# Reordering the first two halves of a fused attention and feed-forward kernel: copies ahead of norms, more banks, selects for the global rows, loads and fills in another order

## The chip, the cores and the metric

The kernel runs on one core of one Trainium2 chip. The metric is device time in microseconds (us) of one execution, lower is better. Within one round of measurements the executions of the kernel before lie within 1.5 to 1.7% of one another. A few executions were of a slower state: one of the kernel before in four of the five rounds of experiments (265.98 to 266.10 us) and one of m9 (269.40 us). Ratios and intervals use the fast ones alone, medians are over all. The rounds ran on different chips; where medians of two rounds are subtracted below, the kernel before moved by under 1 us between them (263.76 to 264.59). Engines are named as in the profile: PE is TensorE, DVE is VectorE, ACT is ScalarE, POOL is GpSimd, SP is SyncE, and SPq or ACTq is the part of an engine that issues DMAs.

## The reference

Windowed attention with a few global keys and a distance bias, followed by a gated feed-forward layer. Cut to what matters:

```python
# q, k, v: (4 batches, 8 heads, 768 positions, 64); n_global = 8; n_local = 96
scores = q @ k.T / sqrt(64)
is_global = key_pos < 8
is_local = (rel >= 0) & (rel < 96)                 # rel = query_pos - key_pos
dist = where(is_global & ~is_local, 96, abs(rel))
scores += -slope[head] * dist                      # slope = 2 ** -(head + 1)
a = softmax(where(is_global | is_local, scores, -1e9))
x = (a @ v) as (3072 tokens, 512)
out = (maximum(x @ w_gate, 0) * (x @ w_val)) @ w_out     # 512 -> 1536 -> 512
```

## The kernel before

A sequence of 768 queries is worked in two halves of 384, so there are eight "halves", numbered here from the first to the eighth (in the code from 0 to 7). Attention of a half goes by four pairs of heads. A helper `weave` lays feed-forward products of one half between attention pieces of a later one. The program is scheduled by hand: the order of these Python calls is the order of each engine's instructions. Some words used below: a *cast* turns float32 into bf16; a *norm* is the last step of a head pair's attention, the product with the inverse of the sum of the exps; a *product* is one tile of a feed-forward layer's first stage, four matmuls; *banks* are the tiles that matmuls write into; *fills* are memsets.

The third half belongs to the second batch, which has value and key buffers of its own (`vbuf[1]`, `kT[1]`). Each value tile starts with the eight global rows. They are loaded once, into tile 0, and then spread to the other tiles by DMAs inside the chip's memory:

```python
def spread_v_globals(b, j0=1, j1=NT):
    for j in range(j0, j1):
        nc.sync.dma_start(out=v_dst(b, 0, NG, j), in_=v_dst(b, 0, NG, 0))

def load_v_half(s):
    b, half = divmod(s, 2)
    if half == 0:
        load_v_globals(b)
        spread_v_globals(b)                 # issued by SP
    for j in range(4) if half == 0 else range(4, NT):
        load_v(b, j)                        # issued by POOL

def load_qk_after(s, by_pairs=False):       # loads that a small DVE memset holds back
    ...
        nc.vector.memset(t[0:1, 0:H:step, 0:1], 0.0)
    ...
```

From the third half on, keys and queries are not transposed by PE but by DMA. POOL casts them, SP issues the transposes, and POOL lays the keys in place:

```python
def early_pieces(s):
    out = [(0.0, lambda p=p: piece_cast_k(s, p)) for p in range(HP)]    # POOL: kc <- ks
    out += [(0.0, lambda n=n: piece_xk(s, n)) for n in range(NN)]       # SP: kN <- kc transposed
    out += [(0.0, lambda p=p: piece_cast_q(s, p)) for p in range(HP)]   # POOL: qz <- qs
    out += [(0.0, lambda n=n: piece_xq(s, n)) for n in range(NN)]       # SP: qT <- qz transposed
    out += [(0.0, lambda p=p: piece_order(s, p)) for p in range(HP)]    # POOL: kT <- kN
    return out
```

The end of the program's setup:

```python
weave(f1_0[G[0]] + f1_0[G[1]], spread(att1, 0.05, 0.95), ...)   # second half's attention
for p in range(HP):
    nc.gpsimd.memset(kT[1][p][...], 0)                          # two of them
nc.gpsimd.memset(vbuf[1][:, NT - 1, :]..., 0)                   # last value tile of batch 1
for j in range(NT):
    fill_ones(nc.gpsimd, 1, j)                                  # ones beside the values
for i in range(2):
    nc.gpsimd.memset(qz[i]..., 0)
load_qk_after(2)
load_w(wo_sb, moe_w_out, 0, DM)
load_v_half(2)                                                  # behind the fills
weave(f1_1[G[0]] + f1_1[G[1]], ...)
weave(f1_0[G[2]] + f1_1[G[2]], spread(early_pieces(2), 0.0, 1.0))
load_qk(3, 0, H)
load_v_half(3)                                                  # behind the transposes
weave(f2_0 + f2_1, spread(attention_pieces(2), 0.0, 0.85), spread(early_pieces(3), 0.2, 0.8))
```

The softmax here doesn't subtract the row's maximum and nothing guards it: scores larger than these inputs give would overflow.

## Time and profile before

| | before |
|---|---|
| time, median of 4 runs beside the changed kernel | 264.59 us (262.21 to 266.27) |
| span of the profiled run, mean granted PE clock | 261.9 us, 0.98 |
| first half's last norm, second half's last norm | 26.22 us, 47.01 us |
| third half: POOL's casts of keys, PE reaches its attention | 56.62 us, 69.59 us |
| gap at 90 us | 2.1 us idle, then 3.2 us at half clock |

Timeline columns: start, duration, engine, line, operation, output<-input, count, and in brackets the idle time ahead and what ended it.

### The profile page before, as it was taken

What the parts mean: (1) busy time and instruction counts of PE and PEld (TensorE: products, weight loads), DVE (VectorE), ACT (ScalarE), POOL (GpSimd) and SP (SyncE); (2) the same over time, 40 slices, a digit from 0 to 9 for tenths busy, and PEclk for the clock granted to TensorE, in tenths of its full rate; (3) what the DMA queues carried; (4) which work ended last, traced back from release to release, by engine and by line L of the source; (5) the groups of instructions that cost most, each with busy time, mean ns of one, the idle gap of its engine ahead of it and who ended that gap; (6) DMA issues with size and microseconds to landing.
All of it is one profiled execution on the core that took longest, in us unless ns stands there. A gap on an engine that the chain in (4) does not pass through costs nothing.

```text
span 261.9 us, 4707 instructions
## 1 busy us (share of the span) xinstructions
PE 240.1 (92%) x1637; PEld 141.6 (54%) x1646; DVE 137.2 (52%) x351; ACT 155.5 (59%) x321; POOL 94.8 (36%) x230
## 2 busy tenths in 40 slices
PE   5664997999998789999999999999999999999994
PEld 2453654566554346655665566655665566556641
DVE  7623796664353337752767167635674366714410
ACT  4165589433477538755776477756875677653321
POOL 8970895026664607710344515800640000000000
PEclk9898899999999979999999999999999999999999
DMA  6999689975994993673753994945681200021012
GB/s 180 183 186 254 148 147 156 185 227 116 245 209 116 189 294 91 138 52 117 240 108 76 125 290 95 144 62 179 183 127 55 80 3 1 3 80 40 0 43 80
DMA packets 82695, 34.36 MB, mean 131 GB/s; under 512 B 58608, under 2 KB 79600, under 8 KB 82672
## 3 DMA queue, kind: packets, MB, share of 16 engines
q1 hardware_dynamic: 50816, 26.16, 37.2%
q0 software_dynamic: 31856, 7.91, 31.1%
q8 instruction: 13, 0.21, 0.3%
q14 instruction: 10, 0.08, 0.1%
HBM read 28.38 MB, written 6.29 MB: 132 GB/s over the span
## 4 chain that ended last, share of the span: by engine, by line
PE 77%; ACT 7%; DVE 7%; DMA 4%; issue 1%; POOL 1%; SPq 1%; POOLq 0%; ACTq 0%
PE ff_ps L472 22%; PE ff_ps L462 21%; PE ff_ps L481 21%; PE qk_ps L366 5%; PE av_ps L394 4%; DMA qT<-qz 2%; DVE xT L411 2%; PE av_ps L425 1%; ACT grelu L465 1%; ACT es L319 1%; DVE ht L474 1%; DMA qs<-in_q_dram 1%; ACT es L369 1%; ACT lnd L435 1%; DMA kN<-kc 1%
## 5 line engine op out<-in xcount | busy, mean ns | idle before, releaser
L472 PE MATMUL ff_ps<-xT,wv 128*128 128x384 bf16 x384 | 78.9, 328 | 0.6 <-DVE ht L474 0.3
L462 PE MATMUL ff_ps<-xT,wg 128*128 128x384 bf16 x384 | 79.3, 330 | 0.0
L465 ACT ACTIVATE grelu<-ff_ps 128x384 bf16<-128x384 f32 x96 | 47.1, 490 | 39.8 <-DVE ht L474 21.0
L474 DVE TENSOR_TENSOR ht<-ff_ps,grelu 128x384 bf16<-128x384 f32 x96 | 53.3, 555 | 27.1 <-PE ff_ps L472 22.6
L481 PE MATMUL ff_ps<-wo_sb,ht 128*128 128x512 bf16 x279 | 66.6, 379 | 0.5
L378 DVE TENSOR_TENSOR es<-es,m_all 128x432 bf16<-128x432 bf16 (+6 forms) x128 | 39.1, 338 | 28.7 <-ACT es L369 28.0
L369 ACT ACTIVATE es<-qk_ps 128x432 bf16<-128x432 f32 (+2 forms) x84 | 43.6, 532 | 12.9 <-PE qk_ps L366 11.5
L472 PEld LDWEIGHTS <-wv 128*128 128x128 bf16 x384 | 36.5, 99 | 23.8 <-issue 2.8
L462 PEld LDWEIGHTS <-wg 128*128 128x128 bf16 x384 | 36.6, 98 | 23.4 <-issue 1.2
L411 DVE TENSOR_TENSOR xT<-av_ps,rcp 64x384 bf16<-64x384 f32 x48 | 26.7, 555 | 43.0 <-ACT rcp L408 38.0
L481 PEld LDWEIGHTS <-ht 128*128 128x128 bf16 x288 | 26.9, 97 | 27.9
L322 POOL CAST kc<-ks 128x384 bf16<-128x384 f32 x24 | 12.3, 555 | 64.5 <-DMA ks<-in_k_dram 64.5
L366 PE MATMUL qk_ps<-qT,kT 128*128 128x432 bf16 (+6 forms) x128 | 28.6, 289 | 2.9 <-DMA qT<-qz 2.1
L403 ACT ACTIVATE lnd<-av_ps 64x384 f32<-64x384 f32 x48 | 23.3, 485 | 10.6 <-PE av_ps L394 10.0
L486 ACT COPY osb<-ff_ps 128x512 f32<-128x512 f32 x24 | 14.1, 586 | 25.3 <-PE ff_ps L481 24.5
L130 POOL DMA_DIRECT2D vbuf<-in_v_dram x28 | 24.3, 876 | 0.8 <-issue 0.7
L394 PEld LDWEIGHTS <-vbuf 128*128 128x128 bf16 x216 | 18.0, 98 | 8.8 <-issue 1.5
L394 PE MATMUL av_ps<-es,vbuf 128*128 128x216 bf16 (+4 forms) x216 | 21.1, 226 | 1.1 <-DVE xT L411 0.8
L366 PEld LDWEIGHTS <-kT 128*128 128x128 bf16 x128 | 12.5, 99 | 12.9 <-issue 2.8
L330 POOL CAST qz<-qs 128x192 bf16<-128x192 f32 x48 | 14.5, 353 | 4.6 <-DMA qs<-in_q_dram 4.4
L408 ACT ACTIVATE rcp<-lnd 128x384 f32<-128x384 f32 x24 | 12.5, 523 | 0.8
L319 ACT ACTIVATE es<-qk_ps 128x432 bf16<-128x432 f32 (+1 forms) x12 | 5.2, 504 | 12.4 <-PE qk_ps L314 12.4
(74 smaller groups left out, 128.5 us busy)
## 6 DMA issues: line engine op xcount, KB each, us to landing
out_dram<-osb SPq DMA_DIRECT2D x24, 256.0 KB
ks<-in_k_dram SPq DMA_DIRECT2D x6, 768.0 KB
qs<-in_q_dram SPq DMA_DIRECT2D x6, 768.0 KB
vbuf<-in_v_dram POOLq DMA_DIRECT2D x24, 120.0 KB, 6.8
ks<-in_k_dram SPq DMA_DIRECT2D x8, 192.0 KB
qs<-in_q_dram SPq DMA_DIRECT2D x8, 192.0 KB
wg<-in_moe_w_gate_dram POOLq DMA_DIRECT2D x3, 512.0 KB, 7.1
wv<-in_moe_w_val_dram POOLq DMA_DIRECT2D x3, 512.0 KB, 9.0
```

What stands on the lines that cost most here:

```text
L130: nc.gpsimd.dma_start(out=v_dst(b, NG + r0, NG + r0 + n, j), in_=v[b, :, KT * j + r0 : KT * j + r0 + n, :].rearrange("h p d -> p h d"))
L366: nc.tensor.matmul(ps[:, c : c + n_], lhsT=kt[:, j, :], rhs=qd[:, :, :, a : a + w], start=True, stop=True)
L369: nc.scalar.activation(es[:, 0:cols], ps[:, 0:cols], AF.Exp, bias=0.0, scale=scale)
L378: nc.vector.tensor_mul(e4, e4, mk)
L394: nc.tensor.matmul(av3[:, :, a : a + w], lhsT=vb[:, j, z0 : z0 + 128], rhs=es[:, c : c + NN * w].rearrange("k (n p) -> k n p", n=NN), star ...
L403: nc.scalar.activation(ln[o0 : o0 + 64], av[d0 : d0 + 64, 0:QH], AF.Ln, bias=0.0, scale=1.0)
L411: nc.vector.tensor_tensor(xT_of[s][r, p, :], av_of[s, p, e_][r, 0:QH], rc[r], op=ALU.mult)
L462: nc.tensor.matmul(psg[:, 0:QH], lhsT=w_of(wg, dc, fc), rhs=xT[:, dc, :], start=(dc == 0), stop=(dc == N_DC - 1))
L465: nc.scalar.activation(gr, psg[:, 0:QH], AF.Relu, bias=0.0, scale=1.0)
L472: nc.tensor.matmul(psv[:, 0:QH], lhsT=w_of(wv, dc, fc), rhs=xT[:, dc, :], start=(dc == 0), stop=(dc == N_DC - 1))
L474: nc.vector.tensor_tensor(ht[:, fc, :], psv[:, 0:QH], st["gr"], op=ALU.mult)
L481: nc.tensor.matmul(ps2, lhsT=ht[:, fc, n * 128 : (n + 1) * 128], rhs=wo_sb[:, fc, :], start=(fc == 0), stop=(fc == N_FC - 1))
```

## The change

Its intent: shorten the chain at the start (masks of the global rows without DVE, casts and copies ahead of the norms, six banks for scores), start feed-forward products before the first half's last norm, and get every load out earlier. The diff, cut to its core:

```diff
-    def setup_global_rows():            # 7 DVE instructions on 8x216, 2 iotas
+    nc.gpsimd.affine_select(...)        # 4 selects write dd[0:NG]
+    def copy_v_globals(eng, b, j0, j1): # first batch: value rows by DVE, no DMA
...
-        banks = [qk_psum.tile(...) for _ in range(3)]
+        pool, name = (ff_psum, "ff_ps") if s == 0 and p % 2 else (qk_psum, "qk_ps")
+        banks = [pool.tile([128, 512], FP32, name=name) for _ in range(3)]
...
-    weave(f1_0[G[0]] + f1_0[G[1]], spread(att1, 0.05, 0.95), [(0.5, lambda: load_w_group(2))])
+    for f in F0[0:3]: f(0, LAST)        # three products all but their last matmul
+    piece_av_wide(0, 3); piece_norm_wide(0, 3)
+    load_w_group(1)
+    for p in range(HP): cast(1, p, P, P)
+    ...                                 # second half's pieces and 9 products by hand
+    load_qk_after(2)
+    for h in (0, 1, 6, 7): setup_mask(h)
+    load_w(wo_sb, moe_w_out, 0, DM)
+    load_v_half(2)                      # now ahead of the fills
     for p in range(HP):
         nc.gpsimd.memset(kT[1][p]..., 0)
     nc.gpsimd.memset(vbuf[1][:, NT - 1, :]..., 0)
+    for i in range(2): nc.gpsimd.memset(qz[i]..., 0)
     for j in range(NT): fill_ones(nc.gpsimd, 1, j)
-    load_qk_after(2)
-    load_w(wo_sb, moe_w_out, 0, DM)
-    load_v_half(2)
-    weave(f1_1[G[0]] + f1_1[G[1]], ...)
-    weave(f1_0[G[2]] + f1_1[G[2]], spread(early_pieces(2), 0.0, 1.0))
     load_qk(3, 0, H)
     load_v_half(3)                      # now ahead of early_pieces(2)
-    weave(f2_0 + f2_1, spread(attention_pieces(2), 0.0, 0.85), spread(early_pieces(3), 0.2, 0.8))
+    weave(f1_1[G[0]] + f1_0[G[1]][4:] + f1_1[G[1]], ..., spread(early_pieces(2), 0.5, 1.0))
+    weave(f1_0[G[2]] + f1_1[G[2]] + f2_0 + f2_1,
+          spread(attention_pieces(2), 0.2, 0.92), spread(early_pieces(3), 0.1, 0.6))
```

## The prediction

> **What bounds the kernel now.** I read the page's slices first, then a table of windows, then the list of waits for the tensor engine (PE), then the timeline around its two worst gaps. The slices are 6.5 us each:
>
> ```profile
> PE   5664997999998789999999999999999999999994
> PEclk9898899999999979999999999999999999999999
> DMA  6999689975994993673753994945681200021012
> ```
>
> From the sixteenth slice on PE is busy 90% or more and its clock is full: the steady state, one half-sequence every 28 us or so, is PE bound, and the change leaves that loop alone. What can be won lies before 96 us: the first four slices (5, 6, 6, 4 tenths), the dip in slices 13 to 15, and the slices with a reduced clock (8 tenths in the second, fourth and fifth, 7 in the fifteenth). The windows (columns: PE, weight load, DVE, ACT, POOL busy us with counts, then clock, DMA share, GB/s) measure it:
>
> ```profile
> 15.00:20.00 5.00, 2.62 (x39) 2.00 (x36) 1.82 (x6) 2.65 (x6) 2.69 (x4) 1.00 1.68 180
> 20.00:25.00 5.00, 2.03 (x28) 1.65 (x29) 2.19 (x9) 2.42 (x7) 0.00 (x0) 0.92 1.21 232
> 26.00:46.90 20.90, 18.41 (x189) 11.42 (x186) 15.61 (x51) 16.48 (x36) 16.16 (x34) 0.96 0.87 155
> 90.00:92.40 2.40, 0.35 (x3) 0.00 (x0) 0.00 (x0) 0.81 (x2) 0.00 (x0) 1.00 1.86 214
> 92.40:95.60 3.20, 3.15 (x11) 1.57 (x12) 1.04 (x3) 0.57 (x1) 0.00 (x0) 0.50 1.64 277
> ```
>
> Three places lose time. First, up to 26 us no engine is full: it is a chain through attention of the first half (cast, transpose, copy, score, exp, value product, norm), one head pair after another. Second, 26 to 46.9 us, where 16 feed-forward products are woven with attention of the second half: PE idles only 2.5 of 20.9 us, but DVE and ACT are near 16. Third, 90 to 95.6 us: PE stands still and then runs at half clock. The waits name the releasers of the first and third:
>
> ```profile
> PE qk_ps L314 <- DVE qT L285: 4.4, 2, 2.5
> PE av_ps L425 <- ACT lnd L435: 3.0, 4, 1.1
> PE qk_ps L366 <- DMA qT<-qz: 2.1, 1, 2.1
> ```
>
> and the timeline shows the first feed-forward product at 26.04 us, taking 1.46 us for its four matmuls where 0.81 is usual (half clock again), the first cast of the second half's keys, which waited for its load, and the third gap: the transposing DMAs of queries were issued at 83.96 us only, because the sync queue issues in order and stood behind an output store (83.52) that waited for its result.
>
> ```profile
> 26.04 1.46 PE L462 MATMUL ff_ps<-xT,wg 128*128 128x384 bf16 x4
> 26.72 0.51 POOL L241 CAST qk<-ks 128x384 bf16<-128x384 f32 x1 [9.04 <-DMA ks<-in_k_dram]
> ...
> 83.52 0.33 SPq L487 DMA_DIRECT2D out_dram<-osb  x1
> 83.96 4.01 SPq L337 DMA_TRANSPOSE qT<-qz  x3
> ...
> 92.45 0.56 PE L366 MATMUL qk_ps<-qT,kT 128*128 128x144 bf16 x2 [2.10 <-DMA qT<-qz]
> 92.80 1.48 PE L472 MATMUL ff_ps<-xT,wv 128*128 128x384 bf16 x4
> ```
>
> **What the Trainium skill says.** "TensorE: Matmul & The Clock Gate", Part 1 (the HAM clock gate): after an idle window of about 3.4 us PE falls to half clock and needs about as long a busy one to return. The trace agrees: 0.50 for the 3.2 us after the gap at 90. So a gap costs itself plus up to half of 3.4 us. "DMA: Bandwidth & Descriptors", Queues, rings and completion order: each DMA engine takes turns between queues, packet by packet. So loads that POOL and SP have both queued share the bandwidth, and an earlier issue brings an earlier share; from 2 to 29 us the DMA never pauses. "VectorE: DVE Perf Modes", Side-by-side: a bf16 copy inside SBUF can run at one to four elements a cycle; no run here shows the new copy of the value rows.
>
> **The change, part by part.**
>
> Masks of the global rows. Seven DVE instructions on 8x216 (4.77 to 7.65 us, some 2.9 us) go; four POOL selects come, by the 0.31 us of an 8x216 iota about 1.3 us, and two iotas go. They sat before the first key copy (7.58 us). In the new order that copy waits for its transposes only: the casts start near 3.7 us (the memset of the new 8x432 source costs DVE about 0.4), keys and queries of two pairs are cast by 6.4, copy of pair 0 from 6.4 (1.35 us, from 7.58 to 8.93 before). Gain about 1.2 us here.
>
> Copies ahead of norms, and banks. Before, copies of pair 2 waited for the norm of pair 0 (DVE idle 3.9 us, then 15.57 norm, 16.05 copy). Now copies 0, 1, 2 run back to back, 6.4 to about 12.3, as the bias products have six banks instead of three and ACT casts pair 2. DVE then casts pair 3 (1 us), spreads the value rows (estimate 0.5 to 1.6 us), and copies pair 3 (14.0 to 15.4). PE keeps program order, so scores of pair 2 stand behind the transposes of pair 3 (13.2). I follow on: exps of pair 2 to 16.2, first ln and reciprocal 17.2, norm 17.9; exps of pair 3 to 18.5; pairs 1 and 2 normed at 20.2 and 21.2; nine early matmuls of three products (9 x 0.163 = 1.5 us at full clock, up to 3 at half); the last pair's norm at 24.9 to 25.5. Then three products need only one matmul each and are done near 25.5 to 26.5; before, the third was done near 28.9. PE is 2.4 to 3.4 us ahead here.
>
> Second half. Key/query loads are issued after the first norm, now about 17.9 against 20.7 us, but share the DMA with the weights; the bytes up to them are the same (6.0 MB by 29 us), so the first cast moves from 26.7 to perhaps 25. Work in the stretch: 9 more products instead of 13 (4 x 0.65 = 2.6 us of PE moved later), the eight mask activations (4.0 us of ACT) leave, two pairs' mask multiplies (2 x 1.3 us of DVE) are replaced by bias products (two pairs, about 0.7 us of PE each). It becomes a latency chain: four copies of 1.56 us, then four rounds of value product, ln, reciprocal, norm, about 2.4 us each while two banks serve. From 25 I reach 44.3 us (44.6 with the first product of the next half), where 13 products are done; before, 16 were done at 47.5, so 13 correspond to 45.5. Most of the earlier lead is thus spent on the chain: gain left about 1 to 2 us. Four masks on ACT then stand before the first ReLU of the next half: minus 0.6.
>
> Queries of the fourth half. Its loads go out before the next weave instead of at 66.5 us, and the early pieces are placed from 0.1 to 0.6 of a weave of 26 us feed-forward work. Its transposes are then issued ten us or more before they are needed. This takes away the idle 2.1 us and the half clock: 3.2 x 0.5 = 1.6 us. Gain 3.7 us.
>
> Third half. Its attention begins about 5 us after the weave starts, near 62 to 63 us; its loads start at 44.4 instead of 48.3 us, and the chain cast to transposes took 13 us before (56.6 to 69.6). But the fourth half's loads (1.6 MB, 5 us at the 330 GB/s of 24 to 28 us) now stand ahead of its transposes in the same queue. I expect a wait of 0 to 2 us, minus 0.7 on average. Spreading attention over more products saves the small waits of 80 to 90 us, perhaps plus 0.7.
>
> Sum: 1.5 - 0.6 + 3.7 - 0.7 + 0.7 = 4.6, rounded up to 4.9 as the start may also be luckier with the clock: 265.9 - 4.9 = 261.0 us.
>
> **Rivals.** (a) The second half is not a chain but stays bound by DVE and ACT busy time (15.6 and 16.5 of 20.9 us). Then taking 2.6 and 4.0 us off them lets most of the 3 us lead through, and the sum is 6 to 8 us: 258 to 260. For it: PE idled just 2.5 us there. Against: at 44 to 47 us PE already waits on ln (1.09 and 0.58 us). (b) The third half's transposes come late behind the new loads: a wait of 2 to 4 us on PE at 62, and the half clock after it, which takes the place of the gap at 90; the sum is 0 to 1.5 us, 264.5 to 266. For it: one queue, in order. Against: all loads are 4 us earlier. (c) The start is held by DMA (share over 1 from 5 to 28 us), so the second half's keys land at 26.7 as before whatever the engines do: the sum falls to about 3.5 us, 262.5. Against: the earlier issue. (d) PE in the first 25 us falls to half clock in the gaps that remain: minus 1 us.
>
> **Range and chances.** The gain at 90 us is the safest term; (a) adds 2 to 3, (b) to (d) take 1 to 4. I put 80% on 257.0 to 264.6 us. Faster by 2% means below 260.6, just under my middle, so the chances are close: 0.46 faster, 0.50 within 2%, 0.04 slower. The three times of before spread over 1%, which widens it.
>
> **What would show it.** Right: no wait of PE on the query transposes near 90 and clock 1.00 there; the first feed-forward matmuls near 21 us and the fourth norm near 25; the second half's last norm at 43 to 45.5 us; PE waiting on ln and norm between 34 and 45. Wrong: a wait of over 2 us on the transposes near 62 (b); first cast of the second half after 26.5 (c); a last norm before 42.5 (a); the steady loop of 28 us per half changed in length.

## More of the kernel before

```profile
35.27 2.72 POOL L601 MEMSET qz<- 128x1536 uint32 x2
...
39.53 3.62 POOL L130 DMA_DIRECT2D vbuf<-in_v_dram  x4
...
56.62 1.86 POOL L322 CAST kc<-ks 128x384 bf16<-128x384 f32 x4 [13.46 <-DMA ks<-in_k_dram]
...
48.33 0.37 SPq L111 DMA_DIRECT2D ks<-in_k_dram  x1
...
50.43 6.18 SPq L126 DMA_DIRECT2D vbuf<-vbuf  x6
58.51 3.91 SPq L333 DMA_TRANSPOSE kN<-kc  x3
62.53 3.94 SPq L337 DMA_TRANSPOSE qT<-qz  x3
...
69.59 0.53 PE L366 MATMUL qk_ps<-qT,kT 128*128 128x432 bf16 x2
```

POOL's memsets are over when it issues the value loads at 39.53, and it waits 13.46 us with nothing behind it that could suffer. What it waits for is the key load that SP issued at 48.33. SP issues the spread of the value rows (L126) behind that load. The transposes go out as soon as the casts are done, and PE comes to the first score product at 69.59 and has no wait in front of it.

## The result, and the profile after

The changed kernel is slower: 276.77 us median of 4 runs (275.21 to 277.85) against 264.59 us. The ratio is 1.0487, with a 95% interval of 1.0374 to 1.0601. (A ratio here is the mean time of one kernel's fast runs over that of the other's of the same rounds, so it is not quite the ratio of the quoted medians.) The outputs were correct within the tolerance. The profiled span went from 261.9 to 273.4 us, 11.5 us longer.

Slices of 6.8 us each show where. Of the page of the changed kernel:

```profile
PE   7475788996069999999999999999999999999994
...
PEclk9999599999659999999999999999999999999998
```

The dip of the slices near 90 us is gone (PE's list of waits has no wait for the fourth half's transposes), but there is a new one in the tenth to twelfth slice (6, 0 and 6 tenths, 61.5 to 82 us), deeper than any in the kernel before, with the clock at 6 and 5 tenths in the last two. The clock is also at 5 tenths in the fifth slice, told of below. Windows of both kernels give its size (columns: PE, weight load, DVE, ACT and POOL busy us with counts, then clock, DMA share, GB/s); first before, then after:

```profile
70.00:80.00 10.00, 9.95 (x63) 5.33 (x63) 4.82 (x14) 7.99 (x18) 4.58 (x12) 1.00 1.24 226
...
90.00:97.00 7.00, 4.90 (x23) 2.42 (x21) 1.43 (x5) 2.52 (x6) 0.00 (x0) 0.76 1.61 273
```

```profile
70.00:80.00 10.00, 2.52 (x8) 1.20 (x9) 1.19 (x2) 0.85 (x2) 7.06 (x24) 0.53 0.52 118
...
90.00:97.00 7.00, 6.73 (x43) 3.62 (x42) 2.56 (x6) 4.56 (x10) 5.42 (x10) 1.00 1.14 145
```

Between 70 and 80 us PE did 8 matmuls where it had done 63, while POOL is the busiest engine. The lists of waits of PE and of POOL in the changed kernel (us in total, times, longest) name both ends of it:

```profile
PE qk_ps L363 <- DMA qT<-qz: 11.3, 1, 11.3
```

```profile
POOL vbuf L634 <- DMA vbuf<-vbuf: 19.0, 1, 19.0
```

The timeline tells how one leads to the other:

```profile
35.03 3.66 POOL L134 DMA_DIRECT2D vbuf<-in_v_dram  x4
...
58.27 0.55 POOL L634 MEMSET vbuf<- 128x544 uint32 x1 [18.96 <-DMA vbuf<-vbuf]
58.77 2.69 POOL L636 MEMSET qz<- 128x1536 uint32 x2
61.41 2.01 POOL L139 MEMSET vbuf<- 128x288 uint32 x7
63.56 2.46 POOL L134 DMA_DIRECT2D vbuf<-in_v_dram  x3
65.99 1.87 POOL L319 CAST kc<-ks 128x384 bf16<-128x384 f32 x4
...
47.55 0.37 SPq L111 DMA_DIRECT2D ks<-in_k_dram  x1
...
49.21 6.14 SPq L126 DMA_DIRECT2D vbuf<-vbuf  x6
55.45 0.39 SPq L111 DMA_DIRECT2D ks<-in_k_dram  x1
57.90 0.37 SPq L111 DMA_DIRECT2D qs<-in_q_dram  x1
67.89 3.91 SPq L330 DMA_TRANSPOSE kN<-kc  x3
71.91 3.94 SPq L334 DMA_TRANSPOSE qT<-qz  x3
...
77.48 0.52 PE L363 MATMUL qk_ps<-qT,kT 128*128 128x432 bf16 x1 [11.34 <-DMA qT<-qz]
```

Read it from the bottom. PE stood from 66.1 to 77.5 us for the query transposes. SP issued them at 71.9 because POOL's casts began at 65.99, not at 56.62 as before. They were that late though the keys had been asked for a little earlier (47.55 against 48.33). POOL was held by its own memset of the last value tile (L634), which in the new order stands behind the spread of the value rows. That tile is a destination of the spread, so the memset has to wait for it. The spread stands on SP behind the loads that a DVE memset holds until the second half's last norm. (That norm is not the only bound: in m2, m3, m6, m10 and m15 below those loads went out at 42.8 to 45.8 us and the spread still started at 48.1 to 51.4, after a wait of 1.6 to 7.5 us for the global rows that it copies.) So POOL did nothing from 39.3 to 58.3 us, and then paid memsets, fills and issues (7.7 us) with everybody waiting, where before they filled time in which POOL was free. The Trainium skill, "TensorE: Matmul & The Clock Gate", gives under Engine queue depths a strict first-in, first-out order for GpSimd (for each of its Q7 cores); the trace agrees, at 18.96 us in which nothing behind the memset ran.

After the hold PE also ran at half clock, 0.52 from 77.4 to 81.0 us, as it did behind the gap at 90 us in the kernel before.

What the prediction said of the first half's norms came true. The four norms of the first half in the changed kernel (L437 in the DVE timeline, last of the four in the fourth line) and the second half's last norm:

```profile
17.29 0.56 DVE L437 TENSOR_TENSOR xT<-av_ps,rcp 128x384 bf16<-128x384 f32 x1 [1.33 <-ACT rcp L434]
...
19.40 0.56 DVE L437 TENSOR_TENSOR xT<-av_ps,rcp 128x384 bf16<-128x384 f32 x1 [1.54 <-ACT rcp L434]
20.34 0.56 DVE L437 TENSOR_TENSOR xT<-qk_ps,rcp 128x384 bf16<-128x384 f32 x1 [0.38 <-ACT rcp L434]
...
23.75 0.56 DVE L437 TENSOR_TENSOR xT<-av_ps,rcp 128x384 bf16<-128x384 f32 x1 [2.27 <-ACT rcp L434]
...
46.88 0.56 DVE L437 TENSOR_TENSOR xT<-av_ps,rcp 128x384 bf16<-128x384 f32 x1 [0.89 <-ACT rcp L434]
```

Against 26.22 us the first half ends 2.5 us earlier. In this profile the second half ends where it did (46.88 against 47.01), with three products fewer done. Its first cast shows a part of why:

```profile
26.32 0.50 POOL L238 CAST qk<-ks 128x384 bf16<-128x384 f32 x1 [8.58 <-DMA ks<-in_k_dram]
```

The loads landed at 26.3 us (26.72 before), although they were asked for 2.8 us earlier (17.90 against 20.72).

This one profile must not be read alone, though. Six of the runs below have the same program up to the second half's last norm. In m2, m3, m5, m10 and m15 it came at 44.50 to 45.12 us, with the first cast at 24.93 to 26.23; in m1 it came at 46.97. PE's mean clock from 24 to 34 us was 0.66 here and 0.83 in m1, and 1.00 in four of the five others (m2: 0.83). The earliest, from m15:

```profile
44.50 0.56 DVE L437 TENSOR_TENSOR xT<-av_ps,rcp 128x384 bf16<-128x384 f32 x1 [0.89 <-ACT rcp L434]
```

So about 2 us of the second half's end differ between executions of the same instructions. They did not decide the result: POOL's hold ends where it does, and the third half's attention starts at 77.51 us in m15 as at 77.48 here.

### The profile page after: what moved, and what is told of

Same layout as the page of the kernel before. It is cut to its first block, busy times and chain, and to the rows that moved or that the text cites.

```text
span 273.4 us, 4719 instructions
## 1 busy us (share of the span) xinstructions
PE 242.1 (89%) x1658; PEld 142.5 (52%) x1667; DVE 135.1 (49%) x339; ACT 157.2 (57%) x323; POOL 93.9 (34%) x229
## 4 chain that ended last, share of the span: by engine, by line
PE 64%; issue 9%; DVE 6%; POOL 6%; DMA 6%; ACT 4%; SPq 4%; POOLq 0%; ACTq 0%
PE ff_ps L459 32%; PE ff_ps L482 22%; PE av_ps L391 5%; PE qk_ps L363 4%; DMA ks<-in_k_dram 3%; DVE xT L408 3%; POOL vbuf L134 2%; SPq L111 2%; SPq L330 1%; DMA qs<-in_q_dram 1%; ACT rcp L405 1%; ACT lnd L400 1%; DVE ht L475 1%; DMA qT<-qz 1%; SPq L334 1%
## 5 line engine op out<-in xcount | busy, mean ns | idle before, releaser
L459 PE MATMUL ff_ps<-xT,wg 128*128 128x384 bf16 x384 | 80.4, 330 | 4.3 <-DVE xT L437 2.9
L366 ACT ACTIVATE es<-qk_ps 128x432 bf16<-128x432 f32 (+2 forms) x78 | 40.9, 531 | 24.3 <-PE qk_ps L363 22.8
L375 DVE TENSOR_TENSOR es<-es,m_all 128x432 bf16<-128x432 bf16 (+5 forms) x118 | 36.4, 340 | 35.4 <-ACT es L366 34.8
L363 PE MATMUL qk_ps<-qT,kT 128*128 128x432 bf16 (+5 forms) x118 | 26.7, 289 | 11.3 <-DMA qT<-qz 11.3
L319 POOL CAST kc<-ks 128x384 bf16<-128x384 f32 x24 | 11.7, 535 | 54.8 <-DMA ks<-in_k_dram 54.8
L400 ACT ACTIVATE lnd<-av_ps 64x384 f32<-64x384 f32 x48 | 23.3, 485 | 12.0 <-PE av_ps L391 11.3
L363 PEld LDWEIGHTS <-kT 128*128 128x128 bf16 x118 | 11.4, 98 | 20.4 <-issue 12.7
L391 PE MATMUL av_ps<-es,vbuf 128*128 128x216 bf16 (+4 forms) x216 | 21.2, 226 | 0.3 <-DVE xT L408 0.2
L316 ACT ACTIVATE es<-qk_ps 128x432 bf16<-128x432 f32 (+2 forms) x12 | 5.5, 531 | 7.0 <-PE qk_ps L311 7.0
```

Of the source, the lines that this page charges most:

```text
L363: nc.tensor.matmul(ps[:, c : c + n_], lhsT=kt[:, j, :], rhs=qd[:, :, :, a : a + w], start=True, stop=True)
L366: nc.scalar.activation(es[:, 0:cols], ps[:, 0:cols], AF.Exp, bias=0.0, scale=scale)
L375: nc.vector.tensor_mul(e4, e4, mk)
L391: nc.tensor.matmul(av3[:, :, a : a + w], lhsT=vb[:, j, z0 : z0 + 128], rhs=es[:, c : c + NN * w].rearrange("k (n p) -> k n p", n=NN), star ...
L400: nc.scalar.activation(ln[o0 : o0 + 64], av[d0 : d0 + 64, 0:QH], AF.Ln, bias=0.0, scale=1.0)
L459: nc.tensor.matmul(st[key][:, 0:QH], lhsT=w_of(w, dc, fc), rhs=xT_of[c][:, dc, :], start=(dc == 0), stop=(dc == N_DC - 1))
```

## The experiments

The theory after reading the trace had three parts. Hold A: POOL's fills behind the spread. Hold B: the fourth half's loads ahead of the third half's transposes on SP's queue (and its value loads ahead of the casts on POOL's), hidden behind A. Hold C: the second half's keys share the DMA with weights, which eats the first half's lead. The rival: the loss is not idle time of PE at 66 to 77 us but work added or slowed elsewhere (the long weave, the ACT casts, the banks). The runs beside which each was timed had medians of the kernel before between 263.76 and 264.21 us.

| run | what it is | median us | ratio | 95% |
|---|---|---|---|---|
| m1 | changed, fills ahead of the value loads | 270.91 | 1.025 | 1.020 to 1.030 |
| m2 | changed, only one memset ahead | 273.18 | 1.034 | 1.028 to 1.039 |
| m3 | changed, fourth half's loads back | 274.01 | 1.037 | 1.032 to 1.042 |
| m4 | before, value loads ahead of the fills | 270.16 | 1.023 | 1.017 to 1.030 |
| m5 | m1 and m3 | 265.18 | 1.002 | 0.997 to 1.007 |
| m6 | changed, weights after the casts | 277.00 | 1.049 | 1.044 to 1.055 |
| m7 | m5 and m6 | 264.44 | 1.002 | 0.997 to 1.007 |
| m8 | first half's part alone, rest of before | 260.71 | 0.988 | 0.984 to 0.993 |
| m9 | m7, third half's attention later | 265.71 | 1.006 | 1.001 to 1.010 |
| m10 | changed, third half's attention later | 274.48 | 1.042 | 1.035 to 1.048 |
| m11 | before, with the selects alone | 265.43 | 1.006 | 1.000 to 1.011 |
| m12 | m8 with the changed kernel's long weave | 271.68 | 1.028 | 1.023 to 1.034 |
| m13 | m9, fourth half's keys laid later | 264.46 | 1.003 | 0.999 to 1.008 |
| m14 | m12, the same | 264.62 | 1.005 | 1.001 to 1.009 |
| m15 | m10, the same | 270.44 | 1.027 | 1.022 to 1.031 |
| m16 | m8, fourth half's transposes earlier | 259.48 | 0.985 | 0.981 to 0.988 |
| m17 | m13, output stores issued by ACT | 267.97 | 1.017 | 1.011 to 1.023 |
| m18 | m16, the same | 264.83 | 1.006 | 1.001 to 1.011 |

### Hold A: the fills behind the spread

**m1**, the changed kernel with the fills ahead of the value loads:

```diff
-    load_w(wo_sb, moe_w_out, 0, DM)
-    load_v_half(2)
     ... memsets of kT[1], vbuf[1], qz and fills of ones ...
+    load_w(wo_sb, moe_w_out, 0, DM)
+    load_v_half(2)
```

> The changed kernel with its GpSimd memsets of the second value buffer, keys and query staging put back ahead of the third half's value loads, as the kernel before has them. Theory A (in-order GpSimd waits 18.96 us at one memset for the spread of the global value rows to land, and casts and transposes of the third half stand behind it): that wait goes, the casts of the third half's keys start when their load lands (54 to 57 us instead of 65.99), PE's wait of 11.34 us on the query transposes falls under 2 us and the half clock after it goes: 276.8 becomes 263 to 265, ratio to before 0.985 to 1.00. Rival R1 (the transposes are held by the fourth half's key and query loads, which now stand ahead of them in the sync queue): the wait stays above 7 us, 271 or more. Rival R2 (attention of the third half is simply placed too early in the weave for its data): the wait falls by under 5 us.

Measured: 270.91 us, 5.9 us below the changed kernel. POOL's wait of 19 us is gone and the casts are at 57.10. But PE still waits 7.5 us, now for keys, because the second hold has come forward. SP's timeline in m1:

```profile
57.50 0.44 SPq L111 DMA_DIRECT2D ks<-in_k_dram  x1
60.73 0.37 SPq L111 DMA_DIRECT2D qs<-in_q_dram  x1
61.20 6.75 SPq L330 DMA_TRANSPOSE kN<-kc  x3
68.06 3.94 SPq L334 DMA_TRANSPOSE qT<-qz  x3
```

The three key transposes were not issued until the fourth half's two loads were (60.73), and took 6.75 us to issue where 3.91 is usual. This is hold B, and only now is it on the path.

**m2** moves only the memset that the trace named:

```diff
     load_qk_after(2)
+    nc.gpsimd.memset(vbuf[1][:, NT - 1, :]..., 0)
     ...
-    nc.gpsimd.memset(vbuf[1][:, NT - 1, :]..., 0)
```

> The changed kernel with only the one memset of the last value tile of the second buffer moved ahead of the value loads; the other memsets, fills and the order of all loads stay. Theory A: the same as with all memsets moved, within 1 us (263 to 266), as only this memset shares bytes with the spread rows; GpSimd shows no wait over 2 us before its memsets. If the mere amount of GpSimd work behind the loads (about 5.5 us of memsets and fills) mattered instead, this run would keep 4 us or more of the loss.

A miss: 273.18 us. The next instruction on the same buffer took over the wait. POOL's waits in m2:

```profile
POOL vbuf L139 <- DMA vbuf<-vbuf: 16.3, 1, 16.3
```

L139 is the fill of ones. It shares no bytes with the spread rows (columns of ones and of values alternate), and yet it waited for them: the wait is for the buffer. Here the trace named the first instruction of a group that waits for the same thing, and moving that one alone won 3.6 us, not the whole.

**m4** is the reverse test: the kernel before, with nothing of the change but these loads ahead of the fills.

```diff
+    load_qk_after(2)
+    load_w(wo_sb, moe_w_out, 0, DM)
+    load_v_half(2)
     ... memsets and fills ...
-    load_qk_after(2)
-    load_w(wo_sb, moe_w_out, 0, DM)
-    load_v_half(2)
```

> The kernel before with nothing changed but the order in GpSimd's queue: the third half's value loads ahead of the memsets, as the change has it (the memset then clears the global rows of one tile of batch 1, so the result may be off, on purpose). Theory A: GpSimd waits for the spread rows to about 58 us, casts of the third half's keys start near 64 to 66 instead of 56.6, and PE, which reaches that attention at 69.6, waits 5 to 9 us: 270 to 275 against 264.6. R1 and R2: nothing moves, within 1 us of before, as the loads of the fourth half and the weave are as before.

Measured: 270.16 us, 6.2 us above the kernel before, with a wait of 20.8 us on POOL:

```profile
59.06 0.55 POOL L600 MEMSET vbuf<- 128x544 uint32 x1 [20.82 <-DMA vbuf<-vbuf]
```

Those six microseconds come from this order alone; no other part of the change is needed for them.

### Hold B: the fourth half's loads ahead of the third half's transposes

**m3** puts those loads back in the changed kernel; **m5** does it on top of m1.

```diff
-    load_qk(3, 0, H)
-    load_v_half(3)
     weave(..., spread(early_pieces(2), 0.5, 1.0))
+    load_qk(3, 0, H)
+    load_v_half(3)
```

> The changed kernel with the fourth half's key, query and value loads put behind the third half's transposes, as before; the memset stays where the change put it. R1: PE's wait on the query transposes falls under 3 us, 265 to 268. Theory A: GpSimd's wait of 19 us stays, PE's wait falls only by the 2.5 us of value-load issues that leave GpSimd's queue there, to 8 to 10 us: 273 to 276, and perhaps a new wait on the fourth half's queries.

> The changed kernel with both orders put back: the memsets ahead of the third half's value loads, and the fourth half's loads behind the third half's transposes. Theory now (two holds in series: GpSimd's wait on the spread rows, and behind it, once it is gone, the fourth half's loads ahead of the transposes on the sync queue; each alone leaves 7 to 11 us of PE waiting): with both gone PE's longest wait on the third half falls under 2.5 us and 7 to 8 us more go than with the memsets alone (270.9): 262 to 264.5, ratio to before 0.99 to 1.00. If a third cause held the transposes, over 5 us of wait would stay. Near 90 us PE should not wait for the fourth half's queries, as its pieces are placed earlier in a longer weave.

Measured: m3 274.01 us with POOL's wait of 19.4 us still there; alone it is worth 2.8 us. Those do not come through SP. In the changed kernel SP had issued the fourth half's two loads at 55.45 and 57.90, ten us before it could issue the transposes (67.89). They come through POOL, where three value loads (2.46 us at 63.56 in the timeline above) no longer stand ahead of the casts, which start at 64.02 and not at 65.99.

On top of m1 the same edit is worth 5.7 us (270.91 to 265.18), and here SP's queue is the reason. In m5:

```profile
57.88 3.92 SPq L330 DMA_TRANSPOSE kN<-kc  x3
67.50 0.34 PE L363 MATMUL qk_ps<-qT,kT 128*128 128x432 bf16 x1 [3.43 <-DMA qT<-qz]
```

Both holds together account for 11.6 (276.77 less 265.18) of the 12.2 us (276.77 less 264.59) between the medians; as ratios, 4.7 of 4.9%. The holds hide one another: with A in place B cost 2.8, without it 5.7.

### Hold C: the second half's loads

**m6** issues a group of weights after the second half's casts and not ahead of them; **m7** does it on top of m5.

```diff
-    load_w_group(1)
     for p in range(HP):
         cast(1, p, P, P)
+    load_w_group(1)
```

> The changed kernel with one edit in GpSimd's queue: the second group of feed-forward weights is loaded after the casts of the second half's keys and queries instead of before. Theory C (the second half is held by its own loads, which share the DMA with 1 MB of weights that are not needed until 41 us): first key cast at 22.5 to 24.5 instead of 26.3, first query cast under 25.5 instead of 28.3, PE's waits on these casts (2.3 us) and its half clock at 26 to 30 us go, the last norm of the second half moves from 46.9 to 43.5 to 45.5. The wait on the third half stays, as GpSimd still waits for the spread rows, and grows where PE arrives sooner, so the total falls little: 273 to 277. Rival D (the second half is a chain through the vector engine whatever the loads do): casts move but the last norm stays within 0.7 us of 46.9.

> Both mended orders and the weights after the casts. Theory C: 1.5 to 3 us below the run with both orders alone (259 to 262), if the third half's data is no later; rival D: within 0.7 us of it.

The mechanism held: in m6 the casts came at 21.87 us and the second half's last norm at 42.09, 4.8 us before that of the changed kernel's profile and 2.4 to 3.0 us before those of m2, m3, m5, m10 and m15. The time did not move, 277.00 and 264.44 us. PE only reached the third half's attention sooner and waited there longer (16.7 us in m6, where POOL's casts still began at 66.56, and 4.7 us in m7). Hold C is real, and it is not where the time went.

### The first half's part alone, and one piece of it

**m8** takes the change up to the early products, with the kernel before from the second half on:

```diff
+    ... the changed kernel's first half, masks 2 to 5 there, six banks, selects ...
+    for f in F0[0:3]: f(LAST, N_DC)
-    weave(f1_0[G[0]] + f1_0[G[1]], spread(att1, 0.05, 0.95), ...)
+    weave(f1_0[3:8] + f1_0[G[1]], spread(att1, 0.05, 0.95), ...)
```

> The first half's part of the change alone (selects for the global rows, copies ahead of norms, score banks, early matmuls of three products, value loads and weights early); second half, weaves and later stages as in the kernel before. By my prediction's own sum for the first half, PE leads by 2.4 to 3.4 us at the third product; of this 1 to 2 us should arrive: 262 to 263.5, ratio 0.988 to 1.0. If the second half is held by its loads (theory C), the lead is eaten: within 1 us of before, ratio 0.996 to 1.004, and the gap at 90 us stays as before.

Measured: 260.71 us, ratio 0.988. The first half's part is a gain of about 3 us, more than the 1.5 us that the prediction had left of it and more than this run's own expectation. Its executions also show a higher granted clock (0.99 to 1.00 against 0.97 to 0.99 of the kernel before beside them), so a part of the gain may be fewer stretches at half clock; that was not taken apart.

**m11** takes only the selects:

```diff
-    nc.gpsimd.iota(pos, ...); nc.gpsimd.iota(relg, ...)
-    setup_global_rows()                      # 7 DVE instructions
+    nc.gpsimd.affine_select(...)             # four, on POOL
```

> The kernel before with the global rows written by selects in place of the seven VectorE instructions, and nothing else of the change. Prediction on record gave the first half's parts together 2.4 to 3.4 us of lead, of which 1.5 was to be left. If VectorE's first stretch is what matters, this alone gives 0.5 to 1.5 us, 262.5 to 263.5 us, ratio 0.994 to 0.998. Rival: the second half is held by its own loads, which land when they land, so the lead is lost there: ratio 0.999 to 1.002.

A miss of both: 265.43 us, ratio 1.006, if anything slower. DVE's copy of the first keys did come 0.55 us earlier (7.03 against 7.58). But POOL issues the value loads behind the selects, and SP the spread behind those loads. The lines of the kernel before, then of m11:

```profile
3.01 0.74 POOL L121 DMA_DIRECT2D vbuf<-in_v_dram  x1
...
7.19 2.35 SPq L126 DMA_DIRECT2D vbuf<-vbuf  x3
```

```profile
4.20 0.74 POOL L121 DMA_DIRECT2D vbuf<-in_v_dram  x1
...
9.16 2.35 SPq L126 DMA_DIRECT2D vbuf<-vbuf  x3
```

The loads went out 1.2 us later and the spread 2.0 us later. PE then waited 1.8 us for it at its first value product, and the first norm came at 16.81 us instead of 15.57. But m4, whose program is the kernel before's up to there, issued that spread at 7.78 and had its first norm at 16.97, so what the selects' wait costs is not settled. In the profiled run PE's clock was also at half from 18 to 31 us, which this one run cannot tie to the wait. In the full change the four selects took POOL 1.9 us, but DVE copies the value rows of the first half and no spread is needed for it (0.67 us on 8x1536).

### Where the third half's attention stands

m5 had repaired both holds and still only equalled the kernel before. It waited 3.4 us at the third half's attention, which the changed weave reaches at 64.1 us and not at 69.6. **m9**, **m10** and **m12** put that attention later:

```diff
-          spread(attention_pieces(2), 0.2, 0.92), ...
+          spread(attention_pieces(2), 0.4, 0.92), ...       # m9, on m7
+          spread(attention_pieces(2), 0.45, 0.92), ...      # m10, on the changed kernel
```

```diff
     # m12, on m8
+    weave(f1_1[G[0]] + f1_1[G[1]], ..., spread(early_pieces(2), 0.5, 1.0))
+    load_qk(3, 0, H); load_v_half(3)
+    weave(f1_0[G[2]] + f1_1[G[2]] + f2_0 + f2_1,
+          spread(attention_pieces(2), 0.42, 0.92), spread(early_pieces(3), 0.1, 0.6))
```

> The repaired kernel with both holds removed and the second half's weights late, with one edit more: the third half's attention pieces are spread over 0.4 to 0.92 of the long weave and not from 0.2. Theory: what is left of the loss there (4.7 us of wait on the queries' transpose near 60 us, and the half clock after it) comes from attention standing in TensorE's order before its data can be there, with feed-forward work behind it that could have been done meanwhile. Then the wait falls under 1.5 us and the time to 258 to 261 us, ratio 0.973 to 0.99. Rival: the work is bounded by the other engines or by the end of the kernel; then the wait goes and the time stays at 263 to 265 us, ratio 0.997 to 1.005.

> The changed kernel as it is, with only the third half's attention pieces later in the long weave (from 0.45). Theory: the loss is TensorE standing idle for data that land near 77 us whatever it does; with some 6 us more of feed-forward work ahead of the wait the wait falls from 11.3 to 4 to 7 us and the time to 268 to 273 us, ratio 1.015 to 1.035. Rival: the loss is work added or lower rate in other stages; then the time stays at 275 to 278 us, ratio 1.04 to 1.055, though the wait shrinks.

> The kernel before with the first half's part of the change (which gave a ratio of 0.988 by itself) and the changed kernel's tail of the weaves: the fourth half's loads after the third half's transposes, its transposes early in the long weave, the third half's attention from 0.42 of it. Theory: the two gains add, 3 us of the first half and some 2 us of the wait at 90 us that is left: 257 to 260 us, ratio 0.973 to 0.985. Rival: the later attention only moves the wait to the end of the weave, where the third half's norms and output must follow: then 260 to 262 us, ratio 0.986 to 0.993.

All three missed: 265.71, 274.48 and 271.68 us. The wait for the transpose in m9 was indeed gone, and another stood in its place; PE's timeline in m9 and in m12:

```profile
80.39 0.22 PE L363 MATMUL qk_ps<-qT,kT 128*128 128x48 bf16 x1 [5.19 <-POOL kT L258]
```

```profile
80.45 0.22 PE L363 MATMUL qk_ps<-qT,kT 128*128 128x48 bf16 x1 [8.32 <-POOL kT L258]
```

L258 is the fourth half's keys being laid into the key tile that both halves share (`put_keys` writes rows of tile 3 for either half). Those pieces are the last of the early pieces, at 0.50 to 0.59 of the weave. By moving attention back I had put them ahead of it in program order, and made the third half wait for the fourth half's data: a dependence of my own making. It was tested in **m13**, **m14** and **m15**, each one of the three with only those pieces behind the products:

```diff
-          spread(early_pieces(3), 0.1, 0.6))
+          spread(early_pieces(3)[:-HP], 0.1, 0.6),
+          [(..., lambda p=p: piece_order(3, p)) ...])       # each behind its pair's products
```

> The kernel of m9 (both holds removed, second half's weights late, third half's attention from 0.4 of the long weave), with one edit: the pieces by which GpSimd lays the fourth half's keys in place come behind the third half's score products in the program, and not ahead of them. In m9's trace the wait had moved from the queries' transpose (4.7 us) to those pieces (5.2 us, released by the second write into the keys). Theory: the fourth key tile is shared by both halves, so placing those pieces ahead of the products made TensorE wait for the fourth half's data; then the wait falls under 1.5 us and the time to 258 to 262 us, ratio 0.975 to 0.992. Rival: after the repairs the third half's data are not the bound and something later is; then the wait goes and the time stays 264 to 266 us.

> The kernel of m12 (first half's part of the change with the long weave, which gave 271.7 us with an 8.3 us wait for the second write into the keys), with the same edit: the fourth half's keys are laid in place behind the third half's score products. Theory of the shared key tile: the 8.3 us wait goes and the time falls by 8 to 12 us, to 259 to 263 us, ratio 0.98 to 0.995. Rival: attention placed that late is itself too late for the norms and the output; then it falls by less than 5 us, to 267 to 271 us.

> The kernel of m10 (the changed kernel with only the third half's attention later, 274.5 us with waits of 6.4 and 3.2 us), with the same edit. Theory that the loss of the changed kernel is TensorE standing idle for data of the third half: the 3.2 us wait goes, the 6.4 us stays, and the time falls to 269 to 272.5 us, ratio 1.02 to 1.033. Rival, that the loss is spread over stages: it stays at 273.5 to 276 us, ratio 1.037 to 1.047.

m15 came out as the theory said: 270.44 us, with the 3.2 us wait gone. It is 4.0 us below m10 for that wait, and with both holds left in it is 6.3 us below the changed kernel. By the weave's own weights the later place puts a quarter of 26 us of products, 6.5 us, ahead of that attention, where PE had stood idle. (The wait shrank by 4.7 us only, from 11.3 to 6.6, since PE came out of the second half earlier in m15's profile.) That speaks against the rival as the cause of the loss. m14 fell by 7.1 us, to 264.62, short of the 8 to 12 expected, and m13 by 1.2 us, a miss. In both the wait for the keys is gone, and a third one came up. In m13 PE waits for a norm, ACT ahead of it for an output store, and SP issues the stores between the transposes (in m14 the wait for that norm is 4.7 us):

```profile
82.15 0.42 PE L391 MATMUL av_ps<-es,vbuf 128*128 128x216 bf16 x4 [3.70 <-DVE xT L408]
...
79.36 0.59 ACT L487 COPY osb<-ff_ps 128x512 f32<-128x512 f32 x1 [3.20 <-DMA out_dram<-osb]
...
72.91 3.81 SPq L330 DMA_TRANSPOSE kN<-kc  x3
76.81 0.52 SPq L488 DMA_DIRECT2D out_dram<-osb  x1
77.45 2.65 SPq L334 DMA_TRANSPOSE qT<-qz  x2
```

**m17** and **m18** let ACT issue those stores, in m13 and in m16 (told next):

```diff
-                nc.sync.dma_start(out=out_v[c, n], in_=osb)
+                (nc.scalar if c < 2 else nc.sync).dma_start(out=out_v[c, n], in_=osb)
```

> The kernel of m13, with one edit: the output stores of the first two halves are issued by ScalarE and not by SyncE, whose queue they shared with the fourth half's transposes. In m13's trace TensorE waits 3.7 us near 82 us for a norm, which waits behind a ScalarE copy into an output buffer that waited 3.2 us for an output store; between 72.9 and 82.2 us the stores stand between transposes that wait for GpSimd. Theory: in-order waiting on SyncE's queue again; then both waits go and the time falls by 3 to 5 us to 259.5 to 261.5 us, ratio 0.984 to 0.992. Rival: the transfers themselves are slow or the issue costs ScalarE as much as the wait did; then 263 to 265 us, ratio 0.999 to 1.005.

> The kernel of m16 (259.5 us) with the same edit. m16 has 1.7 us of the same wait near 80 us, with 1.2 us of ScalarE waiting for an output store. Theory: 1 to 2 us less, 257.5 to 258.7 us, ratio 0.977 to 0.982. Rival: 259 to 260.5 us, ratio 0.983 to 0.988.

Both missed on the wrong side: 267.97 and 264.83 us, 3.5 and 5.4 us slower. ACT's timeline in m17:

```profile
69.80 0.58 ACT L487 COPY osb<-ff_ps 128x512 f32<-128x512 f32 x1 [0.53 <-PE ff_ps L482]
76.59 0.39 ACTq L488 DMA_DIRECT2D out_dram<-osb  x1
77.03 1.64 ACT L366 ACTIVATE es<-qk_ps 128x336 bf16<-128x336 f32 x4 [6.64 <-DMA kN<-kc]
```

The first store was issued 6.2 us after its copy had ended, and ACT stood behind it with the exps that PE needed (a wait of 6.0 us on PE). The trace names a transpose as the releaser in m17 and the fourth half's query load in m18, so what a store on ACT's queue waits for there is not settled. Whether the stores behind transposes are what costs m13 its last few microseconds stays open too, since this way of taking them apart brought a larger wait of its own.

**m16** takes m8, and has only the fourth half's casts and transposes earlier, with its keys laid where they were:

```diff
-          spread(attention_pieces(2), 0.0, 0.85), spread(early_pieces(3), 0.2, 0.8))
+          spread(attention_pieces(2), 0.0, 0.85), spread(early_pieces(3)[:-HP], 0.05, 0.5),
+          spread(early_pieces(3)[-HP:], 0.66, 0.8))
```

> The kernel of m8 (the first half's part of the change with the stages of before behind it, 260.7 us), with the fourth half's casts and transposes at 0.05 to 0.5 of the weave and not 0.2 to 0.65, the laying of its keys where it was. m8 still had TensorE wait 1.9 us for the queries' transpose near 90 us. Theory: that wait goes, and the time falls by 1 to 2.5 us to 258 to 260 us, ratio 0.977 to 0.985. Rival: the transposes then only wait for the fourth half's loads, which stand behind the third half's transposes in the same queue, so the end of the wait does not move: 260 to 261.5 us, ratio 0.985 to 0.992.

Measured: 259.48 us, ratio 0.985 (0.981 to 0.988). There is no wait for the transposes at 90 us any more. The range overlaps with m8's, so the last 1.2 us are likely rather than proven. It is the fastest version seen, 4 us faster than the kernel before: the first half's part of the change, the kernel before's order behind it, and the earlier transposes.

## Why the prediction was wrong

It said 261.0 us, and 276.77 came. By its own steps:

- *First half, "PE is 2.4 to 3.4 us ahead here".* Right, or a little low. The norms were predicted at 17.9, 20.2, 21.2 and 24.9 to 25.5 us and came at 17.29, 19.40, 20.34 and 23.75. The three products were done at 25.0 us, against 29.2 in the profile of before.
- *Selects, "Gain about 1.2 us here".* In the changed kernel the first key copy started at 6.40 us, as predicted. But several edits move it there; by themselves the selects moved it by 0.55 us and gained no time (m11). The working counted DVE's time and not what POOL's queue holds behind the selects: the value loads.
- *Second half, "gain left about 1 to 2 us".* The 44.3 us were nearly right (44.50 to 45.12 us in five of seven profiles), but 13 products were done there at 45.4 to 46.1 us, against the 45.5 that the working gave the kernel before: a gain of about nothing. In the changed kernel's own profile, with PE at half clock, it was a loss. What bounds it is nearer to rival (c) than to the chain of norms: its sign, a first cast after 26.5 us, was missed by little (24.93 to 26.32 us), and earlier loads brought an earlier end (m6). With the order of before behind it, the first half's part is worth 3 us (m8).
- *Queries of the fourth half, "Gain 3.7 us".* The wait and the half clock at 90 us went, as predicted. By itself it was measured only on top of m8, where 1.9 us of wait were left: 1.2 us between the medians (m16). The prediction took from the Trainium skill ("TensorE: Matmul & The Clock Gate", Part 1, the HAM clock gate) that an idle window of about 3.4 us brings the half clock, and made of it an estimate of "up to half of 3.4 us" for what the gap costs behind itself. The trace agrees with the estimate (3.2 us at 0.50, so 1.6 us) and not with the window: PE had stood idle for 2.10 us only.
- *Third half, "I expect a wait of 0 to 2 us, minus 0.7 on average".* **This is the step that failed.** The wait was 11.3 us, and half a clock for 3.6 us came behind it. The working took "the chain cast to transposes took 13 us before", with loads that start earlier, and moved the whole chain forward. (The 13 us were misread too: they end at 69.59 us, where PE came without having to wait, and not where the transposes ended.) It followed SP's queue and did not follow POOL's, where the casts come. It does not mention that the diff swaps value loads and fills, and so did not ask what the fills now stand behind: six DMAs into the same buffer, issued from 49.21 us on. m4 shows that this swap alone costs 6.2 us. Its argument against rival (b), "all loads are 4 us earlier", did not hold either: they started 0.8 us earlier in this profile, 2.5 to 3.2 in those of m2, m3, m10 and m15, and POOL's casts came at 63 to 66 us in all of them.
- *Rival (b).* It had named the right stage and the right consequence, a wait on PE that takes the place of the gap at 90, and one right cause, the fourth half's loads ahead of the third half's transposes in SP's queue. But that cause counts only once A is gone (5.7 us, m5); with A in place the same loads cost 2.8 us by way of POOL (m3). It was sized at 2 to 4 us of wait with no loss in sum, since hold A was missing from it.

The base of the prediction, 265.9 us, was an earlier median of three; beside the changed kernel the kernel before took 264.59. It gave 4% to "slower".

Of the loss, holds A and B explain 11.6 of 12.2 us (m1, m5), and PE's idle time is how they cost it (m15). The repaired kernels m5, m7 and m13 stay 3.7 to 4.5 us above m8. m14 shows where to look: it is m8 with the long weave and nothing else of the second half's part, and at 264.62 us it stands where they do. So the long weave costs about 4 us by itself, about as much as the first half's part gains. Why it does is not settled: each of these kernels has a wait of 3 to 5 us left at the third half or the output stores, and each cure tried brought a wait of its own.

One point was only argued and not tested. In the changed order the memset of the last value tile follows the spread into it, so by the program's text the global value rows of that tile are cleared for the second batch. The same holds for every run that keeps this order (m3, m4, m6, m10 and m15). The outputs stayed within the tolerance all the same, so the check does not see it. A repair of the order, as in m1, is due for that reason as well.

## What to carry to other kernels

Before calling a load "earlier", write down for each engine that the data pass through what stands ahead of them and behind them in that engine's order: a fill that used to cost nothing becomes a hold of 19 us when a DMA into the same buffer comes first, and everything else of that engine waits behind it. Move such things as groups, since the next instruction on the same buffer takes over the wait, and move consumers only with a look at which writes into shared tiles end up ahead of them. When a large change mixes stages, try the stage that reads best alone: the first half's part was worth 3 us all along, under a loss of 12.

## What the Trainium skill lacked or had wrong

- "TensorE: Matmul & The Clock Gate", Engine queue depths, has the strict order of GpSimd's queue, but no figure for what it costs the DMAs that GpSimd is to issue behind other work. Here four selects in place of two iotas put the value loads 1.2 us later and the spread behind them 1.4 to 2.0 us later (m11 against m4 and the kernel before).
- "DMA: Bandwidth & Descriptors", Queues, rings and completion order, does not tell what issuing transposes costs when loads are in flight. Three of them took 3.91 us to issue in the kernel before and 6.75 us right behind two loads of 768 KB each (m1).
- No page that I found says what held a plain store on ScalarE's queue: it was issued 6.2 us after its source was ready, with transposes and loads in flight from SyncE (m17), and 4.3 us in m18.
